# Sigmoid attention and a two-matrix MLP on one core: attention steps at computed places of the second product, and a batch's attention kept within one stream

## The chip, the cores and the metric

The kernel runs on one core of a Trainium2 chip. The metric is the device time of one execution in microseconds; the median over several executions is compared. A core has a matrix engine (TensorE, PE in the profile, with its weight loads shown as PEld), a vector engine (VectorE, DVE), an activation engine (ScalarE, ACT), a general engine (GpSimd, POOL), and a sequencer that only issues transfers and waits (SyncE, SP). Each has its own instruction queue. Transfers are issued from a queue and run beside the engines.

## The reference

Eight batches of twelve heads, 448 positions, head size 64. The attention has a sigmoid in place of the softmax; its output, with the heads side by side, is the input of a two-matrix MLP with a SiLU between (v times its sigmoid).

```python
def _attn_ref(q, k, v) -> np.ndarray:          # q, k, v: (8, 12, 448, 64)
    S = q.shape[2]
    scale = 1.0 / np.sqrt(q.shape[-1])
    scores = scale * np.matmul(q, k.transpose(0, 1, 3, 2)) - np.log(S)
    attn = 1.0 / (1.0 + np.exp(-scores))
    return np.matmul(attn, v).astype(np.float32)

def _moe_ref(x, w_in, w_out) -> np.ndarray:    # x: (3584, 768), w_in: (768, 2048), w_out: (2048, 768)
    h = x @ w_in
    g = h * (1.0 / (1.0 + np.exp(-h)))
    return (g @ w_out).astype(np.float32)
```

The inputs and the output are 32-bit floats; the kernel computes its matrix products on 16-bit floats.

## The kernel before

**Attention.** The twelve heads of a batch are handled in three *quads* of four heads (index i). A quad has seven *steps* (index r), one for each block of 64 key positions: positions are dealt out so that step r holds every seventh one. So a batch has 21 attention steps. A step is `scores` (L175: four matmuls on 64 x 64 parts of the array into the PSUM tile psc, then one sigmoid on ScalarE into attnT, L189) and, later, `values` (L196: four matmuls that add attnT times v to the PSUM tile pav, L204). After a quad's seventh step VectorE writes pav, scaled, into two of the six column blocks of xT (L216), the input of the MLP.

**The operands of attention.** `stage` (L114) loads q and k of a quad from SP's queue into stq and stk; `cast` (L142) brings them to 16 bits on VectorE or GpSimd (L147); then they are transposed, on TensorE with a copy out of PSUM by VectorE (`transpose_pe`, L160, with the transposes at L167 and the copies at L169) for batches 0 and 1, or by a transposing DMA on SP's queue (`transpose_dma`, L156) for later ones. `load_v` (L129), `load_w_in` and `load_w_out` (L98, L108) issue their transfers from GpSimd's queue and change the type on the way. A load with `behind=act` waits for that step's sigmoid.

**The MLP as a stream.** `gemm_stream` (L320) yields the MLP batch by batch. Batch b first has eight `h_pair`s (the first product, two blocks of 128 hidden units in one PSUM tile ph; ScalarE then makes the sigmoid tsig, L274, and VectorE the product gT, L275). Then come its `o_pair`s (the second product, into the PSUM tile po; VectorE scales it into osb, L303 or L308, and SP's queue writes it out, L315): three for even batches, four for odd ones. `products` (L225) cuts a pair into small *steps* of four 64 x 64 matmuls (L234), 12 in an h_pair and 32 in an o_pair. Half way through a pair the row halves change over: a nop on ScalarE's queue (L247) waits for the last matmul of the first half, and the first matmul of the second half waits for the nop. Once no attention is left (batch 7) the matmuls take all 128 rows (L256).

**The order of the work.** The order on each engine is the order in which the program calls, and nothing is rearranged. Batch 0's attention runs alone (L355 to L377), with filler matmuls on zeros (`idle`, L87) between its steps. Every later batch's attention is woven into the stream of the batch before it: the loop at L423 takes one stream step after another and calls `attend` (L407) at some of them. `attend` issues the scores of step n, then the values of step n-2 (LAG), then `side` (L383), which issues the next batch's loads, casts and transposes at fixed step numbers. In an h_pair `attend` comes at share 0.5, and in batch 0 also at the end of the second, fourth and sixth pair. In an o_pair it comes at share 0.5, and besides whenever the steps done fall behind a line that would bring the batch's quota to its end at 0.92 of the o_pairs. The quota reaches two scores into the attention of the following batch.

**PSUM.** psc and the transposes (ptr_qk) of the stream have one buffer (pool ps_sc), pav and the filler one (ps_v), ph and po two (ps_2). In batch 0's own attention the scores alternate between ps_sc and ps_2, and the transposes take a buffer of ps_2.

## Time and profile before

| | |
|---|---|
| median of 14 executions | 402.82 us (401.01 to 404.32) |
| the profiled execution | 404.32 us, of which the profile spans 402.4 us |
| TensorE busy | 381.0 us (95%), 7,900 matmuls |
| ScalarE busy | 226.7 us (56%) |
| VectorE busy | 136.0 us (34%) |
| GpSimd busy | 55.3 us (14%) |
| one attention sigmoid (L189) | 1.008 us, 168 times |
| one tsig (L274) and one gT (L275) | 0.917 and 1.091 us, 64 times each |
| granted TensorE clock | 1.0 over the span |

A line of the timeline gives start, length, engine, source line, operation, out<-in and a count of merged instructions; a bracket holds the engine's idle time before it and what ended that. The chain that ended last is followed back from the last instruction, at each step to what released it. In a table of windows each row is a stretch of time: its length, then the busy time of PE, PEld, DVE, ACT and POOL with the number of instructions, the clock, the DMA share and the rate. Matmuls overlap, and their ends are modelled, so that the distance between two starts says more than a matmul's length.

### The profile page before, as it was taken

To read this page: it belongs to the slowest core of one execution; us is meant where nothing else is said; L and a number is where in the kernel's file an instruction comes from. 1 tells how busy PE (TensorE), PEld (TensorE's weight loads), DVE (VectorE), ACT (ScalarE), POOL (GpSimd) and SP (SyncE) were. 2 spreads that over 40 slices of the span, in tenths; PEclk is the share of its full clock that TensorE was granted. 3 is DMA by queue.
4 is the path that set the end of the run, shared out by engine and by line. 5 is a ranking of instruction groups with operands and counts; after the bars stand their busy time and mean duration, and the time that the engine had idled before them with its cause. 6 is when DMAs were issued, how large, how long until landed. Compare 5 with 4: busy or idle time off the path is not lost.

```text
span 402.4 us, 16786 instructions
## 1 busy us (share of the span) xinstructions
PE 381.0 (95%) x7900; PEld 296.4 (74%) x7900; DVE 136.0 (34%) x140; ACT 226.7 (56%) x234; POOL 55.3 (14%) x69
## 2 busy tenths in 40 slices
PE   8898989899999999899999999998999999999994
PEld 4565667777778778777787798777988777767883
DVE  3443452235322353134322342233521344234311
ACT  3985666557553776657654577656755577624200
POOL 3633001123101111021100111021100000000000
PEclk9999999999999999999999999999999999999999
DMA  7999999799684858297653869287562200130033
GB/s 261 254 249 232 204 213 125 210 215 263 140 129 134 180 118 148 69 199 144 140 102 109 170 128 185 70 187 155 134 101 57 70 3 2 42 80 2 2 81 80
DMA packets 64678, 54.18 MB, mean 135 GB/s; under 512 B 35424, under 2 KB 61024, under 8 KB 64608
## 3 DMA queue, kind: packets, MB, share of 16 engines
q1 hardware_dynamic: 50976, 41.30, 43.9%
q0 software_dynamic: 13632, 11.80, 19.4%
q8 instruction: 62, 1.02, 1.0%
q14 instruction: 8, 0.07, 0.1%
HBM read 45.61 MB, written 11.01 MB: 141 GB/s over the span
## 4 chain that ended last, share of the span: by engine, by line
PE 86%; ACT 6%; DMA 3%; DVE 2%; issue 1%; SPq 0%; POOL 0%; ACTq 0%
PE ph L234 30%; PE po L234 29%; PE psc L185 8%; PE pav L204 7%; ACT attnT L189 6%; PE po L256 5%; PE ph L256 5%; DMA v<-in_v_dram 2%; DMA stk<-in_k_dram 1%; PE pz L93 1%; DVE xT L216 1%; PE ptr_qk L167 1%; DVE gT L275 1%; ACT tsig L274 0%; DVE qT L169 0%
## 5 line engine op out<-in xcount | busy, mean ns | idle before, releaser
L189 ACT ACTIVATE attnT<-psc,bias_s 128x896 f16<-128x896 f32 x168 | 167.5, 1008 | 116.0 <-PE psc L185 115.6
L234 PE MATMUL po<-w_out_sb,gT 64*64 64x384 f16 x3072 | 144.7, 323 | 1.0 <-issue 1.0
L234 PE MATMUL ph<-xT,w_in_sb 64*64 64x448 f16 x2688 | 142.3, 349 | 1.9 <-issue 1.1
L234 PEld LDWEIGHTS <-gT 64*64 64x64 f16 x3072 | 111.2, 107 | 19.9 <-issue 1.4
L234 PEld LDWEIGHTS <-w_in_sb 64*64 64x64 f16 x2688 | 96.0, 107 | 34.2 <-ACTq L247 9.3
L275 DVE TENSOR_TENSOR gT<-ph,tsig 128x896 f16<-128x896 f32 x64 | 69.8, 1091 | 100.2 <-ACT tsig L274 100.2
L274 ACT ACTIVATE tsig<-ph 128x896 f16<-128x896 f32 x64 | 58.7, 917 | 33.9 <-PE ph L234 18.1
L185 PE MATMUL psc<-qT,kT 64*64 64x448 f16 x672 | 65.7, 352 | 7.8 <-ACT attnT L189 6.7
L204 PE MATMUL pav<-attnT,v 64*64 64x448 f16 x672 | 62.6, 350 | 1.2 <-DMA v<-in_v_dram 1.0
L303 DVE TENSOR_SCALAR osb<-po 128x768 f32<-128x768 f32 x26 | 24.9, 958 | 96.3 <-PE po L234 80.3
L185 PEld LDWEIGHTS <-kT 64*64 64x64 f16 x672 | 28.6, 106 | 19.2 <-issue 11.8
L216 DVE TENSOR_SCALAR xT<-pav 128x896 f16<-128x896 f32 x24 | 26.1, 1088 | 42.4 <-PE pav L204 42.4
L147 POOL CAST xq<-stq 128x896 f16<-128x896 f32 x18 | 16.9, 936 | 125.3 <-DMA stq<-in_q_dram 122.7
L204 PEld LDWEIGHTS <-v 64*64 64x64 f16 x672 | 24.8, 107 | 6.5 <-DMA v<-in_v_dram 1.5
L147 POOL CAST xk<-stk 128x896 f16<-128x896 f32 (+1 forms) x25 | 22.6, 906 | 37.3 <-DMA stk<-in_k_dram 29.0
L256 PE MATMUL po<-w_out_sb,gT 128*64 128x384 f16 x256 | 21.0, 326 | 0.0
L256 PEld LDWEIGHTS <-gT 128*64 128x64 f16 x256 | 18.0, 110 | 2.9
L256 PE MATMUL ph<-xT,w_in_sb 128*64 128x448 f16 x192 | 18.5, 353 | 0.0
L256 PEld LDWEIGHTS <-w_in_sb 128*64 128x64 f16 x192 | 12.5, 110 | 5.9 <-issue 0.3
L134 POOL DMA_DIRECT2D v<-in_v_dram x7 | 5.8, 823 | 73.9 <-PE pav L204 53.3
L93 PEld LDWEIGHTS <-zeros 64*64 64x64 f16 x180 | 6.1, 121 | 5.3 <-issue 2.3
L93 PE MATMUL pz<-zeros 64*64 64x448 f16 x132 | 8.3, 353 | 0.0
(27 smaller groups left out, 47.1 us busy)
## 6 DMA issues: line engine op xcount, KB each, us to landing
out_dram<-osb SPq DMA_DIRECT2D x56, 192.0 KB, 2.7
stq<-in_q_dram SPq DMA_DIRECT2D x23, 448.0 KB, 4.3
stk<-in_k_dram SPq DMA_DIRECT2D x23, 448.0 KB, 5.9
v<-in_v_dram POOLq DMA_DIRECT2D x7, 672.0 KB, 10.2
w_in_sb<-in_moe_w_in_dram POOLq DMA_DIRECT2D x8, 384.0 KB, 10.4
w_out_sb<-in_moe_w_out_dram POOLq DMA_DIRECT2D x2, 1536.0 KB, 17.6
v<-in_v_dram POOLq DMA_DIRECT2D x3, 224.0 KB, 6.7
stq<-in_q_dram SPq DMA_DIRECT2D x2, 224.0 KB, 2.7
```

The source lines that it names most:

```text
L93: nc.tensor.matmul(pz[half(t), j, :S], zeros[half(j), :D], zeros[half(j)], start=True, stop=True)
L134: nc.gpsimd.dma_start(v16s[b].rearrange("p t i f -> p (t i) f"), src.rearrange("p t i f -> p (t i) f"))
L147: eng.tensor_copy(x16[:, :, tt, :], st[:, tt].rearrange("p t (r d) -> p r t d", r=R))
L185: nc.tensor.matmul(psc[half(j), t, :S], kT[half(t), r, half(j)], qT[half(t), :, half(j)], start=True, stop=True,)
L189: return nc.scalar.activation(attn[b, i][:, :, r, :], psc[:, :, :S], AF.Sigmoid, bias=bias_s, scale=QKSCALE)
L204: nc.tensor.matmul(pav[half(t), j, :S], v16s[b][half(j), t, i, r * D : (r + 1) * D], attnT[half(j), t, r, :], start=(r == 0), stop=(r == R ...
L216: nc.vector.tensor_scalar_mul(xTs[b][:, 2 * i : 2 * i + 2, :], pav[:, :, :S], SX)
L234: mm = nc.tensor.matmul(out_of(u)[half(c)], lhs(u, k, c)[half(row)], rhs(u, k)[half(row)], start=(ph == 0 and k == 0), stop=(ph == 1 and k ...
L256: nc.tensor.matmul(out_of(u)[half(c)], lhs(u, k, c), rhs(u, k), start=(k == 0), stop=(k == nk - 1),)
L274: nc.scalar.activation(tsig, ph[:, :, :S], AF.Sigmoid, bias=0.0, scale=ISX)
L275: nc.vector.tensor_mul(gTs[b][:, 2 * f2 : 2 * f2 + 2, :], ph[:, :, :S], tsig)
L303: nc.vector.tensor_scalar_mul(osbs[g0].rearrange("p (n e) -> p n e", n=2), po[:, :, :NO2], ISX)
```

## The change

It has these parts. In the stream: the places of the attention steps in the second product are worked out ahead (`places`), so that they are evenly apart with one at each change of row halves; the three additional ones in batch 0's first product are gone; the two lagging steps of values are issued ten stream steps after the last place (`attend_last`), so that a batch's attention ends within one stream; the first score of the following batch is issued at the end of the second product; the very first one ahead of the stream. The numbers at which batch 2's operands, v and w_out are loaded change. In batch 0's attention: values come one step later; the transposes of q and k of a quad stand together, both ahead of their copies; the loads of batch 1's first and third quad are tied to other steps. At the start: k of the first quad is loaded from ScalarE's queue, and the sigmoid that brings in the activation table comes after that issue. At the end: the last output tile is made in pieces of 384, 192 and 192 columns (`o_last`), each with its own copy and its two halves written from two queues.

```diff
--- before.py
+++ after.py
@@ -69,7 +69,6 @@
     bias_s = cpool.tile([P, 1], F32, tag="biass", name="bias_s")
     nc.vector.memset(bias_s, NEG_LOG_S)
     warm = cpool.tile([P, 1], F32, tag="warm", name="warm")
-    nc.scalar.activation(warm, bias_s, AF.Sigmoid)
     ident = cpool.tile([P, P], F16, tag="ident", name="ident")
     make_identity(nc, ident)
 
@@ -122,7 +121,9 @@
             for t in range(0, 2, 1 if split else 2):
                 tn = 1 if split else 2
                 pairs_of = src[b].rearrange("(t i j) (p r) d -> i (j p) t (r d)", t=2, j=2, r=R)
-                dma = nc.sync.dma_start(st[:, t : t + tn], pairs_of[i][:, t : t + tn])
+
+                queue = nc.scalar if split and src is k else nc.sync
+                dma = queue.dma_start(st[:, t : t + tn], pairs_of[i][:, t : t + tn])
                 if behind is not None:
                     tc.add_manual_dep(dma.ins, behind.ins.name, AFTER, reason="order of loads")
 
@@ -160,11 +161,12 @@
     def transpose_pe(b: int, i: int, nms: str, cuts=(0, R), pool=None, tag="ps2"):
         ptr = (pool or ps_2).tile([P, 2, 1024], F16, tag=tag, name=f"ptr_{b}_{i}_{nms}")
         for n, nm in enumerate(nms):
-            xt = new_T(b, i, nm)
             x16 = x16s.pop((nm, b, i))
             for r in range(R):
                 for t in range(2):
                     nc.tensor.transpose(ptr[half(t), n, r * P : (r + 1) * P], x16[:, r, t], ident)
+        for n, nm in enumerate(nms):
+            xt = new_T(b, i, nm)
             for r0, r1 in zip(cuts, cuts[1:]):
                 nc.vector.tensor_copy(
                     xt[:, r0:r1, :],
@@ -314,6 +316,26 @@
                 for s, (bl, r) in enumerate(blocks(g)):
                     nc.sync.dma_start(out_rows[bl, r], osb[half(s)])
 
+    def o_last(g):
+
+        osb = p2.tile([P, DMODEL], F32, tag="osb", name=f"osb_{g}", bufs=4)
+        bl, r = divmod(2 * g, R)
+        cuts = [0, NO2, NO2 + NO2 // 2, DMODEL]
+        for c0, c1, pool, tag in zip(cuts, cuts[1:], (ps_2, ps_sc, ps_v), ("ps2", "pssc", "psv")):
+            po = ps_tile(f"po_{g}_{c0}", pool, tag)
+            for k in range(NFC):
+                for s in range(2):
+                    nc.tensor.matmul(
+                        po[half(s), 0, : c1 - c0],
+                        gTs[bl][:, k, (r + s) * D : (r + s + 1) * D],
+                        w_out_sb[:, k, c0:c1],
+                        start=(k == 0),
+                        stop=(k == NFC - 1),
+                    )
+            nc.vector.tensor_scalar_mul(osb[:, c0:c1], po[:, 0, : c1 - c0], ISX)
+            for s, queue in enumerate((nc.sync, nc.scalar)):
+                queue.dma_start(out_rows[bl, r + s, :, c0:c1], osb[half(s), c0:c1])
+
     def tiles_of(b):
         return range((R * b) // 2, (R * (b + 1)) // 2)
 
@@ -331,15 +353,19 @@
                 todo2 = [[(gs[0], n), (gs[1], n)] for n in range(2)] + [[(gs[2], 0), (gs[2], 1)]]
             else:
                 todo2 = [[(g, 0), (g, 1)] for g in gs]
+            last = todo2.pop()[0][0] if b == B - 1 else None
             for units in todo2:
                 for s in o_pair(units):
                     yield *s, b
+            if last is not None:
+                o_last(last)
 
     stream = gemm_stream()
 
 
 
     stage(0, 0, split=True)
+    nc.scalar.activation(warm, bias_s, AF.Sigmoid)
     idle(11, "start")
     cast(0, 0, "q", nc.vector, split=True)
     cast(0, 0, "k", nc.gpsimd, split=True)
@@ -356,24 +382,23 @@
         nxt = (0, i + 1) if i + 1 < NQ else (1, 0)
         for r in range(R):
             act = scores(0, i, r, ps_2 if (i * R + r) % 2 else None)
-            if r == 0 and i > 0:
+            if r == 1 and i > 0:
                 values(0, i - 1, 0, 4)
-            elif r == 1 and i > 0:
+            elif r == 2 and i > 0:
                 values(0, i - 1, 4, R)
-            elif r == 2:
-                transpose_pe(*nxt, "q")
             elif r == 3:
-                transpose_pe(*nxt, "k")
+                transpose_pe(*nxt, "qk")
                 b2, i2 = (nxt[0], nxt[1] + 1) if nxt[1] + 1 < NQ else (1, 0)
                 cast(b2, i2, "q", nc.vector)
                 cast(b2, i2, "k", nc.gpsimd)
                 load_w_in(i)
                 if i == 1:
                     load_v(1)
-            else:
+            elif r > 0 or i == 0:
                 idle(3, f"{i}_{r}")
-            if (i, r) in ((0, 0), (1, 0), (2, 2)):
-                stage(1, i, behind=act if i else None)
+            for i2, at in enumerate(((0, 0), (1, 0), (2, 5))):
+                if (i, r) == at:
+                    stage(1, i2, behind=act)
     values(0, NQ - 1)
 
 
@@ -386,67 +411,91 @@
         if b == 1:
             if n == 2:
                 load_w_in(3)
-            if n == 7:
+            if n == 4:
                 load_w_out(0)
-            if n == 10:
+            if n == 6:
                 load_w_out(1)
         if b + 1 < B:
+            n_stage, n_v, n_cast = ((11, 14, 17), 15, (14, 17, 20)) if b == 1 else ((0, 4, 8), 3, (6, 10, 14))
             for i2 in range(NQ):
 
-                if n == (8 if b == 1 else 0) + 4 * i2:
+                if n == n_stage[i2]:
                     stage(b + 1, i2, behind=act)
-                if n == (14 if b == 1 else 3) and i2 == 0:
+                if n == n_v and i2 == 0:
                     load_v(b + 1)
-                if n == (12 if b == 1 else 6) + 4 * i2:
+                if n == n_cast[i2]:
                     for nm in "qk":
                         cast(b + 1, i2, nm, nc.gpsimd)
                         transpose_dma(b + 1, i2, nm)
 
-    done = 0
+    s_done = v_done = 0
 
     def attend():
 
-        nonlocal done
-        n = done
-        done += 1
-        act = scores(*steps[n]) if n < len(steps) else None
-        if n >= LAG:
-            b, i, r = steps[n - LAG]
+        nonlocal s_done, v_done
+        step = steps[s_done]
+        act = scores(*step)
+        s_done += 1
+        if s_done - v_done > LAG:
+            b, i, r = steps[v_done]
             values(b, i, r, r + 1)
-        if act is not None:
-            side(*steps[n], act)
-        attending[0] = done < len(steps) + LAG
-
-
-
-    o_pairs = o_quota = o_done = h_pairs = 0
-    while True:
-        s = next(stream, "end")
-        if s == "end":
-            break
-        if not attending[0]:
+            v_done += 1
+        side(*step, act)
+
+    def attend_last():
+
+        nonlocal v_done
+        while v_done < s_done:
+            b, i, r = steps[v_done]
+            values(b, i, r, r + 1)
+            v_done += 1
+
+    def places(n, pairs):
+
+
+        marks = [4, *range(NFC, 2 * NFC * pairs, 2 * NFC)]
+        cuts = [1] * (len(marks) - 1)
+        while 1 + sum(cuts) < n:
+            gaps = [(m1 - m0) / c for m0, m1, c in zip(marks, marks[1:], cuts)]
+            cuts[gaps.index(max(gaps))] += 1
+        at = {marks[-1]}
+        for m0, m1, c in zip(marks, marks[1:], cuts):
+            at |= {m0 + (m1 - m0) * x // c for x in range(c)}
+        return at
+
+
+
+
+    attend()
+    pairs = o_steps = 0
+    for kind, share, b in stream:
+        if b == B - 1:
             continue
-        kind, share, b = s
         if kind == "h":
-            o_pairs, o_done = 0, 0
-            h_pairs += share == 1
-            if share == 0.5 or (b == 0 and share == 1 and h_pairs in (2, 4, 6)):
+            if share == 0.5:
                 attend()
-            if b == 0 and h_pairs in (2, 5) and 0.9 < share < 1:
-
-                i = 1 if h_pairs == 2 else 2
+            if b == 0 and pairs in (2, 5) and 0.9 < share < 1:
+
+                i = 1 if pairs == 2 else 2
                 transpose_pe(1, i, "qk", pool=ps_sc, tag="pssc")
                 if i == 1:
                     cast(1, 2, "q", nc.vector)
                     cast(1, 2, "k", nc.gpsimd)
-            o_quota = min((b + 1) * NQ * R + LAG, len(steps) + LAG) - done
-        elif share < 1:
-            progress = (o_pairs + share) / len(tiles_of(b))
-            if share == 0.5 or o_done < min(o_quota, o_quota * progress / 0.92 - 0.5):
+            pairs = (pairs + (share == 1)) % (NFC // 2)
+            if pairs == 0:
+                o_steps = 0
+                at = places((b + 1) * NQ * R - s_done, len(tiles_of(b)))
+        else:
+            o_steps += 1
+            if o_steps in at:
                 attend()
-                o_done += 1
-        else:
-            o_pairs += 1
+            if o_steps == max(at) + 10:
+                attend_last()
+            if o_steps == 2 * NFC * len(tiles_of(b)):
+                if b + 2 < B:
+                    attend()
+                else:
+                    attending[0] = False
 # ---- launch: one core; inputs and outputs as the reference has them ----
 _INS = ['q', 'k', 'v', 'moe_w_in', 'moe_w_out']
 _OUTS = [((3584, 768), 'float32')]
```

## The prediction

> **What bounds the kernel now.** I read the busy totals first, then the shares of the chain that ended last, then busy time by stage, then the instructions of single stages in order of time. Totals and chain:
>
> ```profile
> PE 381.0 (95%) x7900; PEld 296.4 (74%) x7900; DVE 136.0 (34%) x140; ACT 226.7 (56%) x234; POOL 55.3 (14%) x69
> ...
> PE 86%; ACT 6%; DMA 3%; DVE 2%; issue 1%; SPq 0%; POOL 0%; ACTq 0%
> ```
>
> TensorE sets the end. The 6% of ACT in that chain are moments at which TensorE waits for a sigmoid. A stage table says where. Rows: the stream's first product of batch 0, its second, then first and second of batches 1 and 2; columns: length, then busy time by engine.
>
> ```profile
> 29.70:58.14 28.44, 25.66 (x529) 16.37 (x521) 13.21 (x14) 16.84 (x18) 3.18 (x3) 1.00 1.25 227
> 58.14:81.16 23.02, 21.03 (x486) 17.41 (x481) 5.22 (x7) 12.93 (x13) 4.92 (x6) 1.00 0.82 167
> 81.16:102.51 21.35, 21.35 (x460) 15.67 (x453) 9.59 (x9) 14.48 (x15) 5.96 (x7) 1.00 1.16 231
> 102.51:129.51 27.00, 25.98 (x619) 21.84 (x612) 6.15 (x6) 14.01 (x14) 2.69 (x3) 1.00 0.63 121
> 129.51:150.70 21.19, 21.19 (x456) 15.60 (x449) 9.59 (x9) 14.48 (x15) 3.75 (x4) 1.00 0.69 155
> 150.70:173.15 22.45, 21.15 (x494) 17.33 (x488) 5.19 (x5) 13.94 (x14) 2.69 (x3) 1.00 0.58 124
> ```
>
> From batch 1 on the first product has no gap; the second is about 1 us longer than its busy time, and more is lost inside "busy", since the modelled end of a matmul covers 0.3 us behind it. So I count from starts. TensorE in time order, second product of batch 1:
>
> ```profile
> 105.00 0.39 PE L185 MATMUL psc<-qT,kT 64*64 64x448 f16 x4
> 105.19 0.39 PE L204 MATMUL pav<-attnT,v 64*64 64x448 f16 x4
> 105.38 0.52 PE L234 MATMUL po<-w_out_sb,gT 64*64 64x384 f16 x8
> 106.49 0.38 PE L185 MATMUL psc<-qT,kT 64*64 64x448 f16 x4 [0.59 <-ACT attnT L189]
> ```
>
> Between two attention steps in batch 2's second product, 28 po matmuls run from 156.41 to 157.54, so one is 0.0406 us and a step of the stream (four of them) 0.163. Here 8 po matmuls should take 0.33 and take 1.11: a stall of 0.79. The sigmoid ran from 105.43 to 106.44; the next psc starts at 106.49. **Starts of two psc are therefore never closer than 1.49 us** (60.46 to 61.96 is the same). One attention step is 0.37 on TensorE (105.00 to 105.38), so at seven steps' distance 0.37 + 7 x 0.163 = 1.51 just avoids the wait; 6 loses about 0.15, and 5, 3, 2, 1 lose 0.31, 0.6, 0.8, 1.0 as seen.
>
> **What the skill says.** The Trainium skill, "TensorE: Matmul & The Clock Gate", section "Architectural detail", has ScalarE and VectorE as strict first-in-first-out queues. The trace agrees: the pass-over nop (L247) and the sigmoid that a psc needs can't overtake one another. "ScalarE: Activation LUTs", "Rules for kernel authors": about 0.3 us plus 0.83 ns an element, so 1.04 us for 896; the trace has 1.008, which I use. "DMA: Bandwidth & Descriptors", "Issuing engines are not separate DMA queues": a second issuing engine saves only issue time. The before trace issues from SP and POOL alone, so it does not test that for ScalarE.
>
> **The change, part by part.** Costs against the profiled execution: 404.32 us, span 402.4.
>
> *Even places, batches 1 to 6.* Stalls by counting as above: batch 1 0.79+0.63, batch 2 0.31+0.58+1.02, batch 3 0.79+0.64, batch 4 0.34+0.57+1.02, batch 5 0.84+0.63, batch 6 0.32+0.57; sum 9.05. The new rule puts 12 attention steps at stream steps 4, 10, 16, 22, 28, 35, 41, 48, 56, 64, 72, 80 of a three-pair batch (five distances of 6) and 4, 10, 16, 26, 37, 48, 58, ... 112 of a four-pair one (two of 6). Left over: 3 x 5 x 0.15 + 3 x 2 x 0.15 = 3.15. **-5.9.** Batch 0's second product: 0.47, 0.29 and 0.88 go, 0.75 comes: **-0.9**; a 1.2 us stall at 70 is put down to issue, and stays.
>
> *The two lagging steps are flushed inside the stream, and one score of the next batch ends it.* The matmul count is equal. The flush comes 10 steps (1.6 us) after the last place, later than the 1.49; the xT write (1.09) has six steps (0.98), one psc and four steps of the first product (0.75) before anyone reads it: nothing, and if VectorE is late 1:1. But the closing psc is followed by 24 ph matmuls (1.13) plus 0.19, 1.32 in all before the next: 0.15 lost at six batch starts, **+0.9**.
>
> *First product of batch 0.* It now has 8 attention steps, not 11. Counting starts from 31.5, 3.7 us are stalls. 1.3 of them are here:
>
> ```profile
> 37.47 1.14 PE L234 MATMUL ph<-xT,w_in_sb 64*64 64x448 f16 x20
> 38.78 0.58 PE L167 MATMUL ptr_qk<-ident,xq 128*64 128x128 f16 x14 [0.16 <-ACT attnT L189]
> 40.07 0.58 PE L167 MATMUL ptr_qk<-ident,xk 128*64 128x128 f16 x14 [0.71 <-DVE qT L169]
> ```
>
> The k transposes wait for the copy of q, 0.66 net, twice; with both ahead of the copies that goes. The rest is 0.6 (psc behind the kT copy) and 0.4+0.36 (ph behind sigmoids in pairs). What is queued behind: the copies now start after 28 transposes; two (0.62 each) and the cast xq (1.07) stand ahead of gT of the third pair on VectorE, ending 2.4 us after the transposes; gT takes 1.09, and the fifth pair wants that buffer after 0.19 + 2.65: a new 0.7. With 0.2 at each transposition and 0.2 elsewhere, 1.3 remains: **-2.4**.
>
> *Batch 0's attention.* It is paced by ScalarE, except here:
>
> ```profile
> 14.05 0.39 PE L185 MATMUL psc<-qT,kT 64*64 64x448 f16 x4
> 15.46 0.95 PE L204 MATMUL pav<-attnT,v 64*64 64x448 f16 x16 [1.02 <-DMA v<-in_v_dram]
> 16.25 0.36 PE L185 MATMUL psc<-qT,kT 64*64 64x448 f16 x4
> ...
> 16.66 1.01 ACT L189 ACTIVATE attnT<-psc,bias_s 128x896 f16<-128x896 f32 x1 [0.88 <-PE psc L185]
> ```
>
> The matrix v arrives at 15.4 and ScalarE runs dry for 0.88. With values one step later a further score stands ahead of that wait: ScalarE is covered to about 16.7, and the psc behind pav is ready by 16.45. -0.9; a 0.22 gap at 26.2 behind the split transposition should go too. k by ScalarE's queue: k's first transposes wait 0.28 for the cast; TensorE's filler runs to 5.41 anyway, so the bound is 0 to 0.3, q being slowed by sharing the engines; I take 0.1. The table load (1.28) moves behind two issues (0.45 each) and ends near 3, long before the first sigmoid at 8.4. **-1.2.** The score put ahead of the first product fills part of the 0.65 that it waits for xT: **-0.2**.
>
> *End.*
>
> ```profile
> 396.70 0.49 PE L256 MATMUL po<-w_out_sb,gT 128*64 128x384 f16 x3
> 397.22 0.96 DVE L303 TENSOR_SCALAR osb<-po 128x768 f32<-128x768 f32 x1 [4.24 <-PE po L256]
> 398.21 1.11 SPq L315 DMA_DIRECT2D out_dram<-osb  x2
> ```
>
> Last copy: 958 ns for 768 columns, 552 for 384 (L308), so about 0.3 for 192: -0.65. The second issue goes out beside the first (-0.5), each of 48 KB, not 192 (-0.3). Matmuls of 192 columns should stream in 0.041 each, half the 0.0815 measured for 384 (20.86 / 256); the 14 transposes at 0.041 show that rate with these weight loads. **-1.5.**
>
> Sum: -5.9 - 0.9 + 0.9 - 2.4 - 1.2 - 0.2 - 1.5 = -11.2, or 393.1 for the profiled execution. That one was the slowest of the runs shown; against the median of 402.82 it gives **391.6**.
>
> **Loads that move (bounded).** Batch 2's q and k are staged after attention steps 11, 14, 17 (were 8, 12, 16), v after 15. By my times step 11 falls near 57, step 14 near 61.4. q and k land 4 to 9 us after issue (median 6.7 and 7.5), casts on POOL take 0.94 each, the transposing DMA of k a median 5.7: k about 72 at the usual values, wanted at 74.5, behind it SP's next two loads. v is issued behind those casts, near 65, takes 10, and is wanted at 78. w_out lands 14 and 21 us after 36.3 and 37.5; its issue stands on POOL behind the cast of k for batch 1's third quad, whose load is tied to a score three steps later; I put the halves at 52 and 59, wanted at 53 and 60. Cost: nothing if so, 1:1 if not; I allow 0 to 5 and take 0 for the likeliest. Batch 1's first quad now waits for the first sigmoid, near 9.3 (issued at 5.1 and 6.9 before); behind it on SP stand only loads tied to later scores, and its cast is due near 16, its transposes near 23: nothing. Below nothing is excluded, as none of these holds anyone up now.
>
> **Rivals.**
> (1) The wait moves instead of going. For: 6 is under the 7 that is free, and after the first wait all later steps sit on the edge. If the 84 places cost 0.1 more each, 8.4 of the gain goes: 400. Against: the before trace has dozens of distances of 7 that cost 0.02.
> (2) Late loads at the boundary of batches 0 and 1, as above, 2 to 5 us: 394 to 397. For: slack of 1 to 3 us by medians. Against: batch 2's first load shared the DMA engines with the end of w_out before and would now start after it.
> (3) The stalls go, but the chain is held elsewhere, so that nothing comes: 402 to 403.6. Against: TensorE has 86% of the chain and each stall is in it.
> (4) Slower: kT of batch 2. Every us that it comes after 74.5 holds the in-order TensorE queue for the score that ends the stream, and from 11.2 us late, at 86, the kernel is slower; 405 at 88. It needs 14 us more than the medians, more than the worst landings (9.1, then 9.5) bring.
>
> **Numbers.** Forecast 0.70 (gain 8 to 14.5: 388.3 to 394.8), rival 1 0.13, rival 2 0.08, more than forecast 0.03, rival 3 0.02, rival 4 0.04. The range 387.5 to 397 holds the forecast, rival 2 and the near part of rival 1. This measurement can tell about 0.2%, 0.8 us. Faster 0.94, same 0.02, slower 0.04.
>
> **What would show it.** Right: in the second products no stretch under 24 po matmuls between scores and stalls of about 0.15, 26.4 us in odd batches and 21.7 in even ones (the flush and the closing score add three half steps there), first products near 21.1; batch 0's first product near 24.5; no gap for v near 15; both transposes without a gap; the last copy near 0.3 and less than 4 us from it to the end. Wrong: stalls of 0.3 or more at most places, a wait of psc for qT or kT near 75, of pav for v near 78, or of po for w_out near 53 or 60.

## The result and the profile after

The changed kernel takes 391.52 us (median of 10, 389.98 to 392.26) against 402.79 us: ratio 0.971, 95% interval 0.9691 to 0.9729. The forecast was 391.6. The ratios leave out executions that took over 1.5% longer than the fastest of their kernel; the medians do not. The profiled execution of the changed kernel took 390.94 us, of which the profile spans 389.2. The totals and the chain that ended last, on the page of the changed kernel:

```profile
PE 381.2 (98%) x7944; PEld 294.0 (76%) x7944; DVE 135.1 (35%) x142; ACT 226.8 (58%) x234; POOL 55.2 (14%) x69
...
PE 93%; ACT 3%; DVE 1%; DMA 1%; issue 0%; SPq 0%
```

TensorE's busy time is what it was (381.2 against 381.0); the span around it is 13.2 us shorter, and the moments of ScalarE in the chain went from 6% to 3%. Busy time of the changed kernel by stage, with the rows and columns of the table shown before (first and second product of batch 0, then of batches 1 and 2):

```profile
28.21:52.84 24.63, 24.11 (x513) 16.55 (x505) 12.27 (x14) 15.49 (x16) 3.51 (x4) 1.00 1.21 209
52.84:74.70 21.86, 21.59 (x493) 17.28 (x489) 5.63 (x8) 13.01 (x13) 2.64 (x3) 1.00 0.86 164
74.70:96.10 21.40, 21.36 (x454) 15.58 (x446) 9.21 (x10) 15.48 (x16) 4.51 (x5) 1.00 0.94 190
96.10:122.60 26.50, 26.45 (x626) 23.82 (x621) 6.25 (x7) 12.93 (x13) 5.99 (x7) 1.00 0.87 203
122.60:143.80 21.20, 21.17 (x452) 15.70 (x448) 9.01 (x10) 15.24 (x16) 4.14 (x5) 1.00 0.71 162
143.80:165.40 21.60, 21.59 (x500) 17.46 (x496) 5.74 (x6) 13.18 (x14) 2.30 (x3) 1.00 0.65 124
```

The second products now have next to no gap. A full account of both spans goes by the first start of a ph or po matmul of each stage:

| stage | before, us | after, us | difference |
|---|---|---|---|
| start to the first ph | 29.74 | 28.40 | -1.34 |
| first product, batch 0 | 28.40 | 24.44 | -3.96 |
| second product, batch 0 | 23.02 | 22.05 | -0.97 |
| second products, batches 1 to 6 | 147.80 | 143.49 | -4.31 |
| first products, batches 1 to 6 | 128.86 | 127.48 | -1.38 |
| first product, batch 7 | 18.37 | 18.37 | 0 |
| last second product to the end | 26.25 | 24.94 | -1.31 |

It adds up to -13.3 between two single executions; the medians differ by 11.3. The profiled execution of the kernel before was 1.5 us above its median. Of the first products of batches 1 to 6, 1.6 us are two stalls (0.33 and 1.25) of that execution that the profile puts down to issue (the engine waited for nothing that the profile shows), and so are 1.2 us in the second product of batch 0. The changed kernel's execution has no stall at these places, but nothing in the change is aimed at them.

TensorE in time order in the second product of batch 0 shows what an attention step costs at a distance of six stream steps:

```profile
55.52 0.38 PE L187 MATMUL psc<-qT,kT 64*64 64x448 f16 x4
55.71 0.38 PE L206 MATMUL pav<-attnT,v 64*64 64x448 f16 x4
55.90 1.17 PE L236 MATMUL po<-w_out_sb,gT 64*64 64x384 f16 x24
57.01 0.38 PE L187 MATMUL psc<-qT,kT 64*64 64x448 f16 x4
```

Start of psc to start of psc is 1.49 us once more; the 24 po matmuls need 0.98 of the 1.11 us between 55.90 and 57.01, so 0.13 to 0.15 is lost. That repeats at nearly every distance of 6 in all batches (the last of five loses 0.20).

The attention of batch 0, first TensorE where the wait for v was, then ScalarE over the stage:

```profile
15.04 0.38 PE L187 MATMUL psc<-qT,kT 64*64 64x448 f16 x4 [0.49 <-ACT attnT L191]
15.23 0.95 PE L206 MATMUL pav<-attnT,v 64*64 64x448 f16 x16
```

```profile
8.55 19.03 ACT L191 ACTIVATE attnT<-psc,bias_s 128x896 f16<-128x896 f32 x21 [5.39 <-PE psc L187]
```

All 21 sigmoids run without a gap, and nothing waits for v. The first product of batch 0 around the two transposes, all engines but weight loads and other lines left out:

```profile
36.70 0.58 PE L167 MATMUL ptr_qk<-ident,xq 128*64 128x128 f16 x14
37.09 0.58 PE L167 MATMUL ptr_qk<-ident,xk 128*64 128x128 f16 x14
...
37.71 0.62 DVE L171 COPY qT<-ptr_qk 128x896 f16<-128x896 f16 x1 [1.35 <-PE ptr_qk L167]
...
38.26 0.61 DVE L171 COPY kT<-ptr_qk 128x896 f16<-128x896 f16 x1
...
38.79 1.07 DVE L148 CAST xq<-stq 128x896 f16<-128x896 f32 x1
...
39.78 1.08 DVE L277 TENSOR_TENSOR gT<-ph,tsig 128x896 f16<-128x896 f32 x1
...
40.91 1.33 PE L236 MATMUL ph<-xT,w_in_sb 64*64 64x448 f16 x24 [0.28 <-DVE gT L277]
```

The transposes are back to back. What they displaced is visible too: two copies and the cast stand ahead of gT, and the fifth pair waits for it; by starts that pair takes 2.71 us instead of 2.27. The start of the changed kernel:

```profile
5.41 0.31 PE L167 MATMUL ptr_q<-ident,xq 128*64 128x128 f16 x1
5.50 0.62 DVE L148 CAST xq<-stq 128x448 f16<-128x448 f32 x1 [0.52 <-DMA stq<-in_q_dram]
...
6.17 0.74 PE L167 MATMUL ptr_q<-ident,xq 128*64 128x128 f16 x13 [0.45 <-DVE xq L148]
```

With k loaded beside it, the two halves of q take 3.6 and 4.3 us to land instead of 2.6 and 2.7, and the transposes of q wait. The first psc starts at 8.12, not 7.92. That is one execution of each kernel; the other runs' traces, below with e8, say otherwise. And the end:

```profile
383.25 2.91 SPq L337 DMA_DIRECT2D out_dram<-osb  x3
383.25 2.94 ACTq L337 DMA_DIRECT2D out_dram<-osb  x3
...
385.30 0.36 DVE L335 TENSOR_SCALAR osb<-po 128x192 f32<-128x192 f32 x1 [0.96 <-PE po L328]
```

From the start of the last copy to the end of the span it is 3.9 us, where it was 5.2.

### The profile page after: what moved, and what is told of

Read it like the earlier page. It is cut to its first block, busy times and chain, and to the rows that moved or that the text cites. A ratio compares the mean times of both kernels' runs of the same rounds, so it can differ in the third digit from the quotient of the medians.

```text
span 389.2 us, 16893 instructions
## 1 busy us (share of the span) xinstructions
PE 381.2 (98%) x7944; PEld 294.0 (76%) x7944; DVE 135.1 (35%) x142; ACT 226.8 (58%) x234; POOL 55.2 (14%) x69
## 4 chain that ended last, share of the span: by engine, by line
PE 93%; ACT 3%; DVE 1%; DMA 1%; issue 0%; SPq 0%
PE po L236 32%; PE ph L236 32%; PE psc L187 9%; PE pav L206 8%; PE ph L258 5%; PE po L258 4%; ACT attnT L191 3%; PE po L328 1%; DMA stq<-in_q_dram 1%; PE ptr_qk L167 1%; PE pz L92 0%; DVE xq L148 0%; DVE xT L218 0%; DVE gT L277 0%; DVE kT L171 0%
## 5 line engine op out<-in xcount | busy, mean ns | idle before, releaser
L236 PEld LDWEIGHTS <-w_in_sb 64*64 64x64 f16 x2688 | 92.9, 107 | 34.4 <-ACTq L249 8.1
L206 PE MATMUL pav<-attnT,v 64*64 64x448 f16 x672 | 61.6, 349 | 0.1
L305 DVE TENSOR_SCALAR osb<-po 128x768 f32<-128x768 f32 x25 | 23.8, 953 | 70.2 <-PE po L236 58.5
L258 PE MATMUL po<-w_out_sb,gT 128*64 128x384 f16 x192 | 15.8, 326 | 0.0
L258 PEld LDWEIGHTS <-gT 128*64 128x64 f16 x192 | 13.5, 110 | 2.2
```

What stands on the lines that cost most here:

```text
L206: nc.tensor.matmul(pav[half(t), j, :S], v16s[b][half(j), t, i, r * D : (r + 1) * D], attnT[half(j), t, r, :], start=(r == 0), stop=(r == R ...
L236: mm = nc.tensor.matmul(out_of(u)[half(c)], lhs(u, k, c)[half(row)], rhs(u, k)[half(row)], start=(ph == 0 and k == 0), stop=(ph == 1 and k ...
L258: nc.tensor.matmul(out_of(u)[half(c)], lhs(u, k, c), rhs(u, k), start=(k == 0), stop=(k == nk - 1),)
L305: nc.vector.tensor_scalar_mul(osbs[g0].rearrange("p (n e) -> p n e", n=2), po[:, :, :NO2], ISX)
```

## The experiments

The runs are from several chips, with 402.79, 403.18 or 403.53 us for the kernel before beside them, so ratios to it are compared first. All edits are to the changed kernel unless stated.

| run | edit | median, us | ratio (95% interval) |
|---|---|---|---|
| e1_clustered | places spread as before | 399.46 | 0.9922 (0.9903 to 0.9942) |
| e2_places_alone | the kernel before with new places only | 396.82 | 0.9845 (0.9806 to 0.9883) |
| e3_one_last_copy | last tile as before | 393.04 | 0.9753 (0.972 to 0.9786) |
| e4_close_earlier | closing score two steps earlier | 390.93 | 0.9698 (0.9669 to 0.9726) |
| e5_copy_between | copy of q between the transposes | 395.96 | 0.9832 (0.9798 to 0.9865) |
| e6_values_early | values one step earlier | 393.17 | 0.9747 (0.9714 to 0.9779) |
| e7_values_early_untied | e6, and batch 1's first load untied | 392.99 | 0.9753 (0.972 to 0.9785) |
| e8_k_on_sync | first k from SP's queue | 397.97 | 0.9833 (0.9775 to 0.9891) |
| after_again | none | 393.1 | 0.974 (0.9699 to 0.978) |
| f1_all_distances | a combination | 394.74 | 0.9772 (0.9738 to 0.9807) |
| e9_k_on_sync_less_load | e8, with other loads moved later | 391.48 | 0.9711 (0.9673 to 0.9749) |
| f2_distances_less_load | a second combination | 388.93 | 0.9635 (0.9608 to 0.9663) |

**The places undone, and the places alone.**

```diff
     def places(n, pairs):
-        marks = ...            # evenly, one at each change of row halves
+        at = {
+            3: {4, 11, 16, 24, 31, 38, 45, 48, 58, 72, 79, 80},
+            4: {4, 14, 16, 33, 41, 48, 59, 68, 77, 80, 97, 112},
+        }[pairs]
```

> The changed kernel with one thing undone: in the second products the twelve attention steps stand at places spread as before the change (three pairs: 4, 11, 16, 24, 31, 38, 45, 48, 58, 72, 79, 80; four pairs: 4, 14, 16, 33, 41, 48, 59, 68, 77, 80, 97, 112). The flush, the closing score and all else stay. Theory (two psc starts are never closer than 1.49 us, so short distances cost 1.49 less their own length): stalls of 0.3, 0.6 and 1.0 in each three-pair batch and 0.8 and 0.6 in each four-pair one, 1.91 against 0.82 and 1.40 against 0.30 now; 4 x 1.09 + 3 x 1.10 = 7.7 us more, 399.2. Rival (the gain in the second products comes from keeping a batch's attention within one stream): no difference, 391.5.

Measured 399.46, of 399.2 expected. Groups of instructions, the scores' matmuls of this run; the last columns are TensorE's idle time ahead of them and what ended it:

```profile
L187 PE MATMUL psc<-qT,kT 64*64 64x448 f16 x672 | 65.7, 353 | 10.2 <-ACT attnT L191 8.7 <-DMA kT<-xk 0.5 <-DVE kT L171 0.4
```

and the same line of the changed kernel:

```profile
L187 PE MATMUL psc<-qT,kT 64*64 64x448 f16 x672 | 65.5, 353 | 1.6 <-ACT attnT L191 0.9 <-DVE kT L171 0.4
```

The wait of psc for the sigmoid is 7.8 us larger, and the medians differ by 7.9. By stage, the second products of batches 2, 4 and 6 take 1.2 us more than in the changed kernel and those of batches 3 and 5 take 1.1 more (1.09 and 1.10 expected). The traced execution itself took 402.68 us, more than the median; 1.8 us of that is a wait which has nothing to do with the places and comes up again with e8. The values of batch 1's first step wait for batch 1's v:

```profile
34.38 0.38 PE L206 MATMUL pav<-attnT,v 64*64 64x448 f16 x4 [1.66 <-DMA v<-in_v_dram]
```

The part alone, in the kernel before:

```diff
-        elif share < 1:
-            progress = (o_pairs + share) / len(tiles_of(b))
-            if share == 0.5 or o_done < min(o_quota, o_quota * progress / 0.92 - 0.5):
-                attend()
-                o_done += 1
+        else:
+            o_steps += 1
+            if o_steps in at:      # at = places(quota, pairs), made at the end of the first product
+                attend()
```

> The kernel before with one part of the change: the places of attention in the second products come from the new rule; the two steps of lag across the batch border, batch 0, the first product and the end stay as they were. Thirteen steps go into a batch after batch 0, so a three-pair batch has eight distances of 6 and a four-pair one two. Theory of the 1.49 us distance: 1.64 to 0.8 in batch 0, 1.9 to 1.25 in batches 2 and 4, 0.9 to about 0.8 in batch 6, 1.43 to 0.3 in batches 1, 3, 5: 5.5 us less than before, 397.3. Rival (places don't matter alone): 402.8.

Measured 396.82, 6.0 us under the kernel before. Undone it costs 7.9, alone it brings 6.0, with one score more to place in most batches: more distances of 6 (eight in a three-pair batch). The rival, that keeping a batch's attention within a stream is what helps, falls: e1 keeps that and loses the gain, e2 leaves it out and has most of it.

**The last tile.**

```diff
-            last = todo2.pop()[0][0] if b == B - 1 else None
+            last = None
```

> The changed kernel with the last output tile made as before: two halves of 384 columns, one copy of 768, two writes from one queue. By the prediction's working 1.5 us more (393.0); by the two traces, in which the time from the start of the last copy to the end of the span fell from 5.18 to 3.9 us while the matmuls of the last tile took 0.2 longer, 1.1 more (392.6). Rival (the end is hidden behind something else): no difference.

Measured 393.04, 1.5 more than the changed kernel's 391.52, but the intervals overlap (0.972 to 0.9786 against 0.9691 to 0.9729), and this run's trace has a wait for batch 1's v as well (1.0 us). From the start of its last second product to the end of the span it takes 26.26 us against 24.94. That stage's 1.3 us is the number to go by.

**The closing score.**

```diff
-            if o_steps == 2 * NFC * len(tiles_of(b)):
-                if b + 2 < B:
-                    attend()
-                else:
-                    attending[0] = False
+            if o_steps == 2 * NFC * len(tiles_of(b)) - 2 and b + 2 < B:
+                attend()
+            if o_steps == 2 * NFC * len(tiles_of(b)) and b + 2 == B:
+                attending[0] = False
```

> The changed kernel with the score that closes a stream issued two stream steps earlier (four steps after the flush). Distance to the next score 0.19 + 2 x 0.163 + 1.13 = 1.65 us instead of 1.32. If the 0.25 us lost in the first pair of batches 1 to 6 is the 1.49 us between two psc, it goes: 1.5 us less, 390.0. If it is something else in the change from second to first product (the copy into xT or the weights), it stays: 391.5.

Measured 390.93: the intervals overlap, so the time settles nothing, and the profile must. TensorE at the start of batch 2 in this run:

```profile
123.08 1.33 PE L236 MATMUL ph<-xT,w_in_sb 64*64 64x448 f16 x24
124.21 0.39 PE L187 MATMUL psc<-qT,kT 64*64 64x448 f16 x4
```

By starts the 24 ph matmuls take 1.13 us instead of 1.41, so the wait for the sigmoid is gone. But behind the next psc 0.12 comes back: 0.31 to the next ph instead of 0.19. The row halves change over there, with four psc matmuls (0.19) and no pav to cover it; in f2 below, where a pav stands there too, the 0.12 is gone. Net about 0.1 a batch start from batch 2 on (21.14 instead of 21.23 to 21.27 for the first products), not 0.25.

**The order of transposes and copies.**

```diff
         for n, nm in enumerate(nms):
+            xt = new_T(b, i, nm)
             x16 = x16s.pop((nm, b, i))
             ...                    # 14 transposes
-        for n, nm in enumerate(nms):
-            xt = new_T(b, i, nm)
             ...                    # copy
```

> The changed kernel with the copy of q again between the transposes of q and of k (all five places where both stand together). Theory: in the first product of batch 0 two waits of 0.66 us come back and 0.3 to 0.5 of the wait for gT of the third pair goes; in batch 0's attention ScalarE paces and hides it, or loses up to 0.3 a quad. 0.9 to 1.7 us more, about 392.6. Rival (the transposes were never on the path): 391.5.

Measured 395.96, a good 4 us instead of 0.9 to 1.7. The first product's share came as expected (25.55 against 24.44, with two waits of 0.66 and no wait for gT). The miss is in batch 0's attention, which starts its stream 2.9 us later. ScalarE in time order there:

```profile
8.17 3.70 ACT L190 ACTIVATE attnT<-psc,bias_s 128x896 f16<-128x896 f32 x4 [4.99 <-PE psc L186]
12.72 6.39 ACT L190 ACTIVATE attnT<-psc,bias_s 128x896 f16<-128x896 f32 x7 [0.85 <-PE psc L186]
20.14 6.39 ACT L190 ACTIVATE attnT<-psc,bias_s 128x896 f16<-128x896 f32 x7 [1.03 <-PE psc L186]
27.51 2.80 ACT L190 ACTIVATE attnT<-psc,bias_s 128x896 f16<-128x896 f32 x3 [0.98 <-PE psc L186]
```

A wait inside 28 transposes in one place empties ScalarE once a quad: 0.85 + 1.03 + 0.98 = 2.9. So "both at step 3" pays only together with "both ahead of the copies"; the kernel before had set q and k a score apart.

**The place of values in batch 0.**

```diff
-            if r == 1 and i > 0:
+            if r == 0 and i > 0:
                 values(0, i - 1, 0, 4)
-            elif r == 2 and i > 0:
+            elif r == 1 and i > 0:
```

> The changed kernel with batch 0's values one step earlier, as before the change. By the prediction's working v arrives near 15.4 and ScalarE runs dry: 0.9 us more (392.4). By the trace of the changed kernel v is issued at 5.8 and takes about 5 us, so it is there at 11, since the loads of batch 1's first quad no longer stand ahead of it: then the place of values is worth nothing, 391.5.

Measured 393.17. There is no trace of it that can be read against the others; the next run has the same edit and one more:

```diff
-                    stage(1, i2, behind=act)
+                    stage(1, i2, behind=act if i2 else None)
```

> As the one before, and the loads of q and k of batch 1's first quad are tied to no score, as before the change. If those loads delayed v, it arrives near 15 again, ScalarE has a gap of 0.5 to 0.9 us there and the time is 392.0 to 392.4. If the earlier cast of k alone brought v forward, no gap and 391.5.

Measured 392.99. TensorE and then ScalarE in this run:

```profile
14.75 0.95 PE L206 MATMUL pav<-attnT,v 64*64 64x448 f16 x16 [0.35 <-DMA v<-in_v_dram]
...
17.66 0.57 PE L92 MATMUL pz<-zeros 64*64 64x448 f16 x8 [1.01 <-DVE xT L218]
```

```profile
18.66 1.01 ACT L191 ACTIVATE attnT<-psc,bias_s 128x896 f16<-128x896 f32 x1 [0.81 <-PE psc L187]
...
26.02 1.01 ACT L191 ACTIVATE attnT<-psc,bias_s 128x896 f16<-128x896 f32 x1 [0.65 <-PE psc L187]
```

Two things. v is waited for again, with a landing 8.7 us after its issue at 5.96, where the changed kernel's, issued at 5.82, lands 5.3 after: tying batch 1's first loads to a score is what brought v forward by 3.6 us. The other traces agree: 8.3 to 8.8 us wherever those loads are untied (the kernel before, e2, e7), 5.1 to 6.4 wherever they are tied. And the edit made a wait that neither kernel has. The filler now at step 2 needs pav's one buffer and waits for the copy into xT, and ScalarE runs dry for 0.81 and 0.65. With three gaps of 0.2 that is 2.1 us, and the stream starts at 30.99 instead of 28.40. The times don't show that loss: both ratios lie by the 0.974 that the changed kernel itself has in its second measurement (after_again). So e6 does not measure the place of values by itself, and how much that place alone is worth stays open; with v there at 11 the trace leaves it nothing to cover.

**The queue of the first k.**

```diff
-                queue = nc.scalar if split and src is k else nc.sync
+                queue = nc.sync
```

> The changed kernel with the first k loads issued from SP's queue behind q again. By the trace of the changed kernel the second half of q is late (its cast ends at 6.1 instead of 4.5) and the first psc starts at 8.12 instead of 7.92: 0.2 us less here, 391.3. By the prediction 0.1 us more. A difference of that size shows in the start of the first psc alone.

Both expectations failed: 397.97 (one of six at 392.38, the rest 397.31 to 399.85). The place is the first product of batch 0, 28.73 us instead of 24.44. TensorE there:

```profile
32.84 0.36 PE L187 MATMUL psc<-qT,kT 64*64 64x448 f16 x4
35.83 0.51 PE L206 MATMUL pav<-attnT,v 64*64 64x448 f16 x4 [2.63 <-DMA v<-in_v_dram]
36.12 4.05 PE L236 MATMUL ph<-xT,w_in_sb 64*64 64x448 f16 x48
```

and its busy time in the 3.4 us behind the wait (the number before the DMA share is the granted clock):

```profile
36.00:39.40 3.40, 3.40 (x40) 1.75 (x36) 0.00 (x0) 0.78 (x1) 1.98 (x2) 0.50 1.24 207
```

The first pav of batch 1 waits for batch 1's v: 2.8 us by starts. The idle stretch then costs a second time, because TensorE gets half its clock for 3.4 us; the 48 ph matmuls, 2.27 in an undisturbed pair, take 3.88. Together 4.4. The Trainium skill, "TensorE: Matmul & The Clock Gate", section "What's actually happening", describes a gate that halves the clock after an idle window of about 3.4 us and opens again after a busy one of that length. The trace agrees in the 0.50 and in the 3.41 us for which it lasted (35.96 to 39.37). It differs in what set it off: the wait was shorter than 3.4 us, and between 32.8 and 36.0 TensorE was busy for 0.57. The 1.8 us of e1 and the 1.0 of e3 at the same place were followed by no half clock.

Why v is late: k's cast on GpSimd ends 1.4 us later (7.3 instead of 5.9), and the loads of v, of w_in and of batch 1's v are issued behind it on the same queue. The two transfers of w_in just ahead of batch 1's v land at 28.0 and 30.4 instead of 26.0 and 28.0. Batch 1's v is issued at 20.36 (19.63 in the changed kernel), takes 15.4 us instead of 12.4, and lands at 35.78 instead of 32.05. The changed kernel wants it at 32.77: slack 0.7. The kernel before wanted it at 35.77 and had it at 34.2.

The later issue is the smaller part (0.7 of 3.7), and the queue of k is not all of it. With k on ScalarE's queue as well, the time that batch 1's v takes to land varies by more than the slack: 11.1, 12.4, 12.6, 13.7 and 14.8 us in after_again, the changed kernel, e4, e3 and e1, which are the same program up to there. Three of these five waited for v, by 0.4 (after_again), 1.0 (e3) and 1.8 us (e1). What sets that time is not shown.

At the start itself this run speaks for the prediction: its first psc is at 8.35, later than 8.12. Over all traces it starts at 7.73 to 8.25 (and once at 9.17) in the eight with k on ScalarE's queue, median 8.05, and at 7.92 to 8.35 (and once at 9.03) in the five with k on SP's, median 8.20.

Is that wait all of it? The next run keeps k on SP's queue and takes another load out of v's way:

```diff
-            for i2, at in enumerate(((0, 0), (1, 0), (2, 5))):
+            for i2, at in enumerate(((0, 0), (1, 0))):
...
             if n == 2:
+                stage(1, 2, behind=act)
                 load_w_in(3)
...
-                if i == 1:
-                    cast(1, 2, "q", nc.vector)
-                    cast(1, 2, "k", nc.gpsimd)
+            if b == 0 and pairs == 4 and 0.9 < share < 1:
+                cast(1, 2, "q", nc.vector)
+                cast(1, 2, "k", nc.gpsimd)
```

> The changed kernel with the first k loads on SP's queue, and with the loads of batch 1's third quad tied to a score of the stream (step 2 of batch 1, some 7 us later) and its casts two pairs later, so that they don't share the DMA engines with batch 1's v. If the 4 to 7 us that k on SP's queue alone cost are the wait of the first pav of batch 1 for v (2.6 us in its profile, then half the TensorE clock for 3.4 us), v is there by about 33 to 34, the clock stays at 1.0 there, and the time is near the changed kernel's: 391 to 392. If the cost is elsewhere (the start itself), it stays at 396 to 398.

Measured 391.48. TensorE at the same place:

```profile
33.49 0.36 PE L187 MATMUL psc<-qT,kT 64*64 64x448 f16 x4
33.68 0.36 PE L206 MATMUL pav<-attnT,v 64*64 64x448 f16 x4
```

No wait, clock 1.00, first product of batch 0 in 23.73; v is issued at 20.15, hardly earlier than in e8, but lands at 32.6. The start was no better than in e8 (first psc at 9.03), so the loss was the wait for v and the clock behind it, not the start.

**The changed kernel again, and two combinations.**

> The changed kernel once more, as the measure for the kernel that runs beside it on the same chip: 391.5.

Measured 393.1 at a ratio of 0.974. In this profile the first psc starts at 9.17. q landed 0.25 us later than in the changed kernel's first profile, but most of the delay is TensorE's clock: the 14 transposes of k stand 54 ns apart by starts, not 30, and the profile's first record of the full clock is at 10.52 instead of 6.53. Batch 1's v was waited for by 0.4 us by starts. The margin at batch 1's v is thin.

```diff
-                at = places((b + 1) * NQ * R - s_done, len(tiles_of(b)))
+                extra = 1 if b % 2 == 1 and b + 2 < B else 0
+                at = places((b + 1) * NQ * R + extra - s_done, len(tiles_of(b)))
```

(with the closing score of e4, the queue of e8, and a flush that stops at the batch's end)

> The changed kernel with the closing score two steps earlier, the first k loads on SP's queue, and one more score of the following batch in the streams of four pairs (batches 1, 3, 5), which leaves eleven places with two distances of 6 for those of three pairs (batches 2, 4, 6). By the 1.49 us distance: 6 x 0.25 and 3 x 0.5 and 0.2 less than the changed kernel, 3.2 in all: 388.3. If moved scores bring new waits (for xT or pav at the border), 390 or more.

The first combination (the closing score earlier, k on SP's queue, and one score more in the streams of batches 1, 3 and 5) missed: 394.74. The places did their part (three-pair second products 20.64, 20.65 and 20.54 us instead of 21.5), but with k on SP's queue batch 1's v came at 36.5, 3.7 us late by starts, and the half clock behind it, again for 3.41 us: the first product of batch 0 took 29.61. So the cause of e8's loss shows a second time, though v was issued at 18.84 here, earlier than in the changed kernel. The second combination has the edits of f1 and of e9, both without the one to k's queue.

> The changed kernel with the closing score two steps earlier, one more score of the following batch in the streams of batches 1, 3 and 5, and the same later loads of batch 1's third quad; k stays on ScalarE's queue. By the places: 0.6 from the closing score, 3 x 0.87 - 3 x 0.16 = 2.1 from the places (as the profile of the earlier combination shows them), 0.5 from gT of the third pair, which no cast delays any more: 388.3 if v of batch 1 is not waited for. 390 or more if the moved loads are late themselves.

Measured 388.93, ratio 0.9635 with an interval (0.9608 to 0.9663) below both of the changed kernel's (0.9691 to 0.9729, and 0.9699 to 0.978): faster than the changed kernel. TensorE at the start of its batch 2:

```profile
122.40 0.39 PE L187 MATMUL psc<-qT,kT 64*64 64x448 f16 x4
122.58 0.52 PE L236 MATMUL po<-w_out_sb,gT 64*64 64x384 f16 x8
122.91 1.33 PE L236 MATMUL ph<-xT,w_in_sb 64*64 64x448 f16 x24
```

Eight po matmuls now stand between the closing score and the first product. The first product of batch 0 fell to 23.73 (no cast ahead of gT), the second products of batches 2, 4 and 6 to 20.5 to 20.6.

## Why the prediction was right, point by point

- *Even places.* Right in mechanism and size: stalls left over are 0.3 in four-pair and about 0.8 in three-pair batches, where the prediction had 0.30 and 0.75. e1 and e2 show it from both sides. Rival 1, a wait that moves to the other places, did not come: distances of 7 and more lose nothing (28 po matmuls take 1.14 us). The -5.9 stands against -4.31 in the stage table for two reasons. Counted in half steps (the four matmuls of a score or of its values, 0.19), each second product takes on one more and that of batch 6 two, 1.3 us in all, so that the stalls fell by 5.6; and about 0.5 us of stalls fell into batch 1's second product (26.66 against 26.18 in batches 3 and 5), part of it put down to issue. The sentence that "the flush and the closing score add three half steps there" was wrong for these batches: it holds in batch 0 alone.
- *Batch 0's second product.* -0.9 predicted, -0.97 measured, and the agreement is chance. The three half steps more cost 0.56, which the prediction left out here, and the 1.2 us stall that was to stay is not in the changed kernel's execution, where 0.4 stands at the start of the stage.
- *Closing score.* +0.9 predicted. The wait is there, but larger (0.25 a batch start, not 0.15): the sigmoid behind the closing psc of batch 1 starts 0.54 us after that psc, where 0.43 was measured before, and the two psc are 1.60 apart. And e4 shows that moving it returns only 0.1 of it.
- *First product of batch 0.* -2.4 predicted for stalls. The stage lost 3.96, of which 0.9 is five half steps moved elsewhere: -3.0. The stall for gT was mis-sized (0.44, not 0.7), the waits at the transposes right. What e5 adds: in batch 0's attention the wrong order costs 2.9 once both transposes stand together, which no term of the prediction named.
- *Batch 0's attention.* The gain came (ScalarE without a gap; -1.34 up to the first ph, -1.4 predicted), but the step "with values one step later a further score stands ahead of that wait" was not what removed the wait: v lands at 11.1, not 15.4. Of these 4.3 us, 1.0 is an earlier issue, behind an earlier cast of k, and 3.3 that batch 1's first loads no longer go ahead of it. The prediction had costed that tie at nothing and did not connect it with v.
- *k by ScalarE's queue.* The total hid an error here. At the start the -0.1 may well be right: the two profiled executions show +0.2, the medians over all traces (8.05 against 8.20) about -0.15, and neither is clear of the scatter. What the prediction missed lies 25 us later, on batch 1's v: with the rest of the change in place, taking the queue back costs 4 to 5 us (0.9833 against 0.974 and 0.971). The list of late loads checked batch 2's v, q and k and w_out, and left out batch 1's v, whose slack was 0.7 us in the changed kernel's profile and less than nothing in e1, e3 and after_again. The half clock behind a long wait was no term of the prediction either.
- *End.* -1.5 predicted, -1.3 by stage. The last copy took 0.36, not 0.3; the prediction's own two lengths give 0.35 for 192 columns (552 less half of 958 - 552). The matmuls of 192 columns came at 0.041 each by starts, as predicted, though the evidence for it was misread: the 14 transposes, of 128 columns, start 0.03 apart, and 0.041 is their stretch with the modelled end in it. The last copy starts 5.47 us after the tile's first matmul, 5.43 before, so the pieces cost next to nothing, not the 0.2 that e3's expectation has. The rest of the gain, about 0.75, comes with the smaller last writes and the second queue, which no run separates.
- *Late loads at batches 0 and 1, rival 2; rival 4.* No wait for qT, kT or v of batch 2 near 75 to 78. The casts of batch 2's first quad ran near 62.5 and 65, as worked out. kT landed at 73.6 and was wanted at 74.7; the first half of w_out landed at 52.2 and was wanted at 52.8.

The mechanism of the largest term was right and is shown. That the total was right to 0.1 us is luck: the sum of -11.2 was made for the profiled execution, where -13.3 came; the second measurement of the changed kernel gave 393.1; and errors cancelled. The first product of batch 0 gained 0.6 more than allowed, the closing scores cost 0.6 more, half steps were miscounted, and the profiled execution of the kernel before held 2.8 us of issue stalls that the changed kernel's did not repeat.

## What to carry to other kernels

When two engines feed one another through one buffer, measure the shortest distance from start to start (here 1.49 us) and count the work between any two places; a greedy rule that meets a fixed place makes short distances, and each cost about the difference here. When a stream of work gets faster, list every load that the faster part will want earlier, in the order of slack, and look at what stands ahead of it in its issuing queue and what is under way beside it. A slack is worth only what the landing time leaves of it: here 0.7 us of slack stood against landing times from 11.1 to 14.8 us of one and the same load, and the queue of a 448 KB operand, many issues earlier, or a load beside it (e9, f2) bore on whether it was waited for. The long waits of TensorE, 2.8 us in e8 and 3.7 in f1, were paid for twice.

## What the runs showed of the hardware that was not expected

In e8, after TensorE had been almost idle for 3 us (0.57 us busy in 3.2), it ran at half clock for 3.41 us, at a cost of 1.6 us on top of a wait of 2.8. f1 has the same, 3.41 us behind a wait of 3.7; waits of 1.0 and 1.8 us in e3 and e1 had no such effect.

Loading k beside q brought the first half of k forward (its cast started at 4.19 instead of 5.72) and q back (landings of 3.6 and 4.3 us instead of 2.6 and 2.7). The later of the two gained: the last of the four casts ends at 6.0 to 6.5 us in the eight traces with k on ScalarE's queue and at 6.9 to 8.0 in the five with k on SP's. Little of that reaches the first score.

In one profile of the changed kernel and in e9 the first score came late (9.17 and 9.03 against 7.7 to 8.4). The first had TensorE at half speed for longer (transposes 54 ns apart, not 30, up to 10.52); in e9 the second half of k landed at 7.40, 0.7 us later than in e8, whose loads up to there are the same. Why either happened stays open.

The nop of a half change-over does not stand behind the running sigmoid: in the profile of the kernel before, 16 of the 80 end while a ScalarE instruction is under way, as the one at 105.94 to 105.96 does inside the sigmoid from 105.43 to 106.44. In that of the changed kernel none does.
